# Joined row-tiled runs, one run per kind in the second layer, and another ready rule for an engine's own results

## The chip, the cores and the metric

The kernel runs on one core of a Trainium2 chip. The metric is the time of one execution in microseconds on the device, the median of several runs. The clock of TensorE (PE) has two levels, 1.2 and 2.4 GHz; the profile shows what was granted in each stretch.

## The reference

What is computed is an attention through packed queries, followed by two feed-forward layers:

```python
def sm_attn(qq, kk, vv):
    s = scale * np.matmul(qq, kk.transpose(0, 1, 3, 2))
    s = s - np.max(s, axis=-1, keepdims=True)
    a = np.exp(s)
    a = a / (np.sum(a, axis=-1, keepdims=True) + 1e-09)
    return np.matmul(a, vv)
p_packed = sm_attn(p, k, v)              # q, k, v: (8, 8, 576, 64); p: (8, 8, 32, 64)
out = sm_attn(q, p_packed, p_packed)
x = out.transpose(0, 2, 1, 3).reshape(4608, 512)
h = x @ moe_w_in;  g = h * np.tanh(np.log1p(np.exp(h)));  x = g @ moe_w_out     # 512 -> 2048 -> 512
h = x @ moe2_w_in; g = h - np.tanh(h);                    y = g @ moe2_w_out    # 512 -> 2048 -> 512
```

## The kernel before

The weights come as 64-bit words; ScalarE (ACT) and VectorE (DVE) decode them (`dec_unit`, `dec_split`, `dec_pair`) into float32 and split each into a high and a low part, so that a product of float32 precision is three matmuls (`PASSES`). The first layer's weights are decoded at the start, the second layer's (32 steps, `w2_step` apart) beside the first layer, and parked in DRAM (`w2i_d`, `w2o_d`).

**Attention** (`attention`, per batch b of 8): first scores (`scores`, L484, two calls j), transposes (L511, L513), the packed values (L532, L540), then second scores for each half hf of the 576 tokens (`second_scores`, L558), whose soft-max (L563 to L585, on DVE and ACT) leaves the tile `a2[b, hf]`. `mix(b, g)` (L614, g from 0 to 3) multiplies the packed values into a quarter of the first weights; ACT (L620) and DVE (L622) copy the result from PSUM into the tile `m`. The matmuls of L484, L558 and L614 use 64 rows and 32 columns of the array each, four column tiles beside each other: they are called row-tiled here. Everything after is on the full 128 by 128 array.

**First layer** (`layer1`, 128 steps n): two products of six matmuls of 288 columns (L648, from `m` and `a2`), mish on ACT (L652), the split (L654 on ACT, L655 on DVE into `g`), and 24 matmuls of 288 columns into four accumulators (L666).

**Second layer** (`pair2` and `second`, 72 pairs n in 9 blocks of 512 tokens): seven products of six matmuls of 256 columns (L784), from combinations of blocks of weights (`wm`, two tiles of pool `m` per pair, of 4 and 3 products) and of activations (`yq`), in three PSUM banks `ba`, `bb`, `bc`. Copies (L795 on ACT) and adds (L798 on DVE) make the two hidden tiles `hb`; the last part of the second comes by ACT (L815). `second` takes each through a chain on ACT and DVE (L824 to L840) into `g` and 12 matmuls of 512 columns into the accumulators (L850), evicted by L856 after the sixteenth.

**What sets the order.** `Plan` collects all operations with a key, a duration and their buffers, and `emit` walks through modelled time: each engine takes the ready operation with the lowest key whose buffers are free. The program's order on each engine is what comes out; on the chip each engine follows it, waiting where it must. The ready time of an operation is the end of what it waits for plus `LAT` (0.14 us in the model). All row-tiled and product banks come from one pool `bk` of four PSUM banks. In `pair2` a slot is a fifteenth of `TP`, and the first hidden tile's accumulation stands two `TP` behind its pair.

Of the kernel before, what the change touches and what calls it, by code (L numbers as in the profile page):

```python
# [70 lines left out]
class Plan:  # L71


    LAT = 0.14
    TABLE = 1.3
    WINDOW = 3.413

# [3 lines left out]
    def op(self, eng, dur, fn, key, deps=(), take=(), give=(), table=None):  # L81
        o = Op()
        o.table = table
        o.eng, o.dur, o.fn, o.key = eng, dur, fn, key
        o.takes, o.gives, o.outs, o.ready, o.end = list(take), list(give), [], 0.0, None
        o.wait = 0
        o.seq = len(self.ops)
        for b in o.gives:
            b.left += 1
        for d in set(x for x in deps if x is not None):  # L90
            d.outs.append(o)
            o.wait += 1
        self.ops.append(o)
        return o

    def emit(self):
# [17 lines left out]
        while left:  # L114
# [7 lines left out]
            while moved:  # L122
                moved = False
                for e in engs:
# [9 lines left out]
                    while avail[e]:  # L134
                        ent = heapq.heappop(avail[e])
                        need, turn = {}, True
                        for b in ent[2].takes:
                            for k in (b.kind, b.cap):
                                if k is not None:
                                    need[k] = need.get(k, 0) + 1  # L140
                                    turn = turn and (k.queue is None or k.queue[0] is b)
                        if turn and all(len(k.free) >= n and k not in held_kinds for k, n in need.items()):
                            pick = ent[2]
                            break
                        held_kinds.update(k for k, n in need.items() if len(k.free) < n)
# [44 lines left out]
                    for d in o.outs:  # L190
                        d.wait -= 1
                        d.ready = max(d.ready, o.end)
                        if d.wait == 0:
# [20 lines left out]
def tile_packed_attention_mish_tanhshrink(  # L214
# [70 lines left out]
    def ka(n):  # L285
        return T0 + n * TA
# [84 lines left out]
    w2_st = {}  # L371
    w2_step = (ka(102.7) - ka(11.22)) / 32

# [56 lines left out]
    for i in range(32):  # L430
        key = ka(11.22) + i * w2_step
        if i < 16:
# [9 lines left out]
    a2, a2_rd = {}, {}  # L442
    pp, pp_rd = {}, {}

    def attention(b):
# [3 lines left out]
        if b:  # L449
            spans = [(ka(8.5), ka(12.5), 26) if b == 1 else (ka(16 * b - 16) + 20.02, ka(16 * b - 8) + 8.64, 26)]  # L450
            spans += [(ka(16 * b + 8 * hf - 8) - 13.96, ka(16 * b + 8 * hf) - 21.81, 14) if b > 1 else
                      (ka(12 + 2 * hf), ka(14.5 + 2.5 * hf), 14) for hf in range(2)]
# [23 lines left out]
        def scores(j):  # L476
# [4 lines left out]
            def f():  # L481
                for hf in range(2):
                    for c in range(4):
# [3 lines left out]
                            kk[c][0].tile[64 * j:64 * j + 64, hf * HALF:(hf + 1) * HALF], start=True, stop=True)  # L487
            s1 = op("PE", 1.19, f, key(2), [pt_ld] + [x[1] for x in kk], sc, [pt] + [x[0] for x in kk])
            for hf in range(2):
# [55 lines left out]
        def second_scores(hf):  # L545
# [14 lines left out]
            mm = op("PE", 1.19, f, key(2), [pp_rd[b]] + [x[1] for x in qq], st + [ex, fx, a], [x[0] for x in qq] + [pb])  # L560
            for j in range(2):
# [34 lines left out]
    def mix(b, g):  # L596
# [14 lines left out]
        def f():  # L611
            for j in range(2):
                for c in range(4):
                    T.matmul(pm[j].tile[32 * c:32 * c + 32, :], pp[b].tile[64 * j:64 * j + 64, 32 * c:32 * c + 32],  # L614
                             ws[c][2]()[64 * j:64 * j + 64, :], start=True, stop=True)
        z = op("PE", 1.94, f, k0, [pp_rd[b]] + [w[1] for w in ws], pm + [m], [w[0] for w in ws] + [pp[b]])
        for j in range(2):
# [145 lines left out]
    def pair2(n, sw):  # L763
# [33 lines left out]
        def add(half, tok, bk, c, slot, deps, take, give):  # L797
# [3 lines left out]

        p1 = product(0, 0, ba, [act2[0]], [ba], True)
        s1 = copy(c1, ba, 1, [p1])
        p2 = product(1, 1, bb, [], [bb], True)
        c11 = add(0, 0, bb, c1, 2, [p2, s1], [hb[0]], [bb, c1])
        p5 = product(2, 2, bc, [], [bc], True)
        s5 = copy(c5, bc, 3, [p5])
        p6 = product(3, 5, ba, [p1, s1], [], False)
        sy = copy(cy, ba, 6, [p6])
        p3 = product(4, 6, bc, [p5, s5], [], False)  # L810
        c12 = add(0, 1, bc, cy, 7, [p3, sy, c11], [], [bc, cy])
        p7 = product(5, 9, ba, [p6, sy], [], False)
        c22 = add(1, 1, ba, c5, 10, [p7, s5], [hb[1]], [c5])
# [120 lines left out]
```

## Time and profile before

| | us |
|---|---|
| median of 3 runs | 1515.66 |
| the runs | 1515.66, 1519.52, 1515.3 |
| the profiled execution | 1519.44 |
| its span, first to last instruction | 1517.6 |
| PE busy (matmuls) / weight loads | 1485.4 / 1340.3 |
| DVE busy | 1044.0 |
| ACT busy | 1003.6 |

Matmuls are pipelined, so that a busy PE is not a PE at its peak: how fast it goes is read from the distance between the starts of its groups in the timeline. The idle time of an engine stands in brackets with what ended it. In the table of stages the columns are the stretch, its length, and the busy time with the number of instructions for PE, weight loads (PEld), DVE, ACT and POOL, then the granted share of PE's full clock, the share of the DMA engines and GB/s.

### The profile page before, as it was taken

To read this page: it belongs to the slowest core of one execution; us is meant where nothing else is said; L and a number is where in the kernel's file an instruction comes from. 1 tells how busy PE (TensorE), PEld (TensorE's weight loads), DVE (VectorE), ACT (ScalarE), POOL (GpSimd) and SP (SyncE) were. 2 spreads that over 40 slices of the span, in tenths; PEclk is the share of its full clock that TensorE was granted. 3 is DMA by queue.
4 is the path that set the end of the run, shared out by engine and by line. 5 is a ranking of instruction groups with operands and counts; after the bars stand their busy time and mean duration, and the time that the engine had idled before them with its cause. 6 is when DMAs were issued, how large, how long until landed. Compare 5 with 4: busy or idle time off the path is not lost.

```text
span 1517.6 us, 28157 instructions
## 1 busy us (share of the span) xinstructions
PE 1485.4 (98%) x11112; PEld 1340.3 (88%) x11112; DVE 1044.0 (69%) x1916; ACT 1003.6 (66%) x1992; POOL 0.2 (0%) x4
## 2 busy tenths in 40 slices
PE   4999999999999999999999999999999999999999
PEld 1888899898989989899998898989898898989987
DVE  6978472745646433331488889797988888797876
ACT  5896665666566645543576767676777777676765
POOL 0000000000000000000000000000000000000000
PEclk9899999999999999999999999999999999999999
DMA  8788492655757242312965656565556657575551
GB/s 285 248 301 294 151 300 88 227 189 181 245 167 250 100 148 64 94 62 72 349 213 198 199 174 225 180 224 184 201 195 209 198 181 232 167 231 172 192 194 52
DMA packets 100084, 289.73 MB, mean 191 GB/s; under 512 B 10224, under 2 KB 27760, under 8 KB 90736
## 3 DMA queue, kind: packets, MB, share of 16 engines
q1 hardware_dynamic: 99952, 287.94, 56.4%
q8 instruction: 87, 1.43, 0.4%
q14 instruction: 45, 0.37, 0.1%
HBM read 241.76 MB, written 46.14 MB: 190 GB/s over the span
## 4 chain that ended last, share of the span: by engine, by line
PE 94%; DMA 3%; ACT 2%; DVE 1%; issue 0%; SPq 0%; ACTq 0%
PE acc L850 26%; PE acc L666 26%; PE bk L784 24%; PE bk L648 14%; PE bk L614 2%; PE bk L484 1%; DMA st<-in_w1i 1%; PE bk L532 1%; DMA st<-in_w1o 1%; PE bk L558 1%; DMA x<-in_v 1%; DMA m<-w2i_d 1%; PE bk L511 0%; DMA xw<-w1i_d 0%; ACT st L312 0%
## 5 line engine op out<-in xcount | busy, mean ns | idle before, releaser
L850 PE MATMUL acc<-g,wo 128*128 128x512 f32 x1728 | 444.4, 393 | 0.0
L666 PE MATMUL acc<-g,wo 128*128 128x288 f32 x3072 | 436.6, 296 | 0.4 <-DVE g L655 0.4
L666 PEld LDWEIGHTS acc<-g,wo 128*128 128x128 f32 x3072 | 414.3, 188 | 16.1 <-issue 14.6
L850 PEld LDWEIGHTS acc<-g,wo 128*128 128x128 f32 x1728 | 306.6, 189 | 50.1
L784 PEld LDWEIGHTS bk<-yh,m 128*128 128x128 f32 x2160 | 292.3, 191 | 20.6 <-DVE x L798 2.5
L784 PE MATMUL bk<-yh,m 128*128 128x256 f32 x2160 | 306.7, 284 | 0.1
L648 PEld LDWEIGHTS bk<-a,m 128*128 128x128 f32 x1536 | 212.4, 190 | 35.7 <-ACT a L584 9.4
L648 PE MATMUL bk<-a,m 128*128 128x288 f32 x1536 | 231.2, 300 | 10.5 <-ACT a L584 8.5
L655 DVE TENSOR_TENSOR g<-e,g 128x576 fp32r<-128x576 f32 x128 | 96.6, 755 | 202.7 <-ACT g L654 196.4
L652 ACT ACTIVATE e<-bk 128x288 f32<-128x288 f32 x256 | 103.4, 411 | 140.6 <-PE bk L648 139.9
L835 DVE TENSOR_TENSOR tt<-x,tt 128x512 f32<-128x512 f32 x144 | 99.3, 690 | 68.3 <-ACT tt L828 68.2
L824 ACT ACTIVATE e<-x 128x512 f32<-128x512 f32 x144 | 90.8, 630 | 67.7 <-DVE x L798 66.3
L795 ACT ACTIVATE pc<-bk 128x256 f32<-128x256 f32 x216 | 75.5, 374 | 71.8 <-PE bk L784 70.6
L784 PEld LDWEIGHTS bk<-a,m 128*128 128x128 f32 x864 | 113.3, 191 | 8.7 <-DMA m<-w2i_d 2.9
L784 PE MATMUL bk<-a,m 128*128 128x256 f32 x864 | 115.6, 283 | 2.7 <-DMA m<-w2i_d 2.7
L829 DVE SCALAR_TENSOR_TENSOR xw<-xw,xw 128x512 f32<-128x512 f32 x144 | 99.4, 690 | 25.6 <-ACT xw L827 23.9
L837 DVE COPY_PREDICATED xw<-e,tt 128x512 f32<-128x512 uint32 x144 | 109.3, 759 | 1.6
L798 DVE TENSOR_TENSOR x<-bk,pc 128x256 f32<-128x256 f32 x216 | 90.0, 418 | 24.0 <-PE bk L784 23.6
L839 ACT ACTIVATE g<-xw 128x512 fp32r<-128x512 f32 x144 | 89.4, 621 | 23.9 <-DVE xw L837 23.5
L840 DVE TENSOR_TENSOR g<-xw,g 128x512 fp32r<-128x512 f32 x144 | 98.8, 686 | 7.6 <-ACT g L839 7.6
L825 ACT ACTIVATE xw<-e,c_qb 128x512 f32<-128x512 f32 x144 | 102.3, 711 | 0.0
L833 DVE SCALAR_TENSOR_TENSOR xw<-xw,x 128x512 f32<-128x512 f32 x144 | 98.6, 685 | 0.0
(105 smaller groups left out, 1254.7 us busy)
## 6 DMA issues: line engine op xcount, KB each, us to landing
m<-w2i_d SPq DMA_DIRECT2D x72, 1024.0 KB, 5.1
m<-w2i_d SPq DMA_DIRECT2D x72, 768.0 KB, 4.4
xw<-w1i_d SPq DMA_DIRECT2D x112, 256.0 KB, 4.5
w2i_d<-x SPq DMA_DIRECT2D x56, 256.0 KB, 3.9
x<-in_k SPq DMA_DIRECT2D x32, 288.0 KB, 5.5
x<-in_q SPq DMA_DIRECT2D x64, 144.0 KB, 4.0
y_d<-yv SPq DMA_DIRECT2D x16, 576.0 KB, 4.1
out_t<-x SPq DMA_DIRECT2D x36, 256.0 KB, 5.3
```

What stands on the lines that cost most here:

```text
L648: T.matmul(h.tile[:, :HALF], r(m.tile[:, fc % 4, kc, wl, :]), r(x.tile[:, kc, al, :]), start=(i == 0), stop=(i == 5))
L652: fr.append(op("ACT", a_cost(HALF, True), lambda c=c, h=h: A.activation(e.tile[:, c, :], h.tile[:, :HALF], AF.Mish), kf + 1, [g1] + fr, [e ...
L655: lo = op("DVE", v_cost(576), lambda: V.tensor_tensor(out=r(gt.tile[:, 1]), in0=e.tile, in1=gt.tile[:, 0], op=ALU.subtract), kf + 1.2, [hi ...
L666: T.matmul(ac.tile[:, :HALF], r(wo[fc].tile[:, wl, oc * 128:(oc + 1) * 128]), r(gt.tile[:, gl, c, :]), start=(fc == first and i == 0), sto ...
L784: T.matmul(bk.tile[:, :HB], r(wv[:, kc, wl, :]), r(yq[blk, j].tile[:, kc, yl, :]), start=(first and i == 0), stop=(i == 5), skip_group_che ...
L825: p1 = op("ACT", a_cost(TB, False, True), lambda: A.activation(s1.tile, zz.tile, AF.Sigmoid, bias=c_qb, scale=Q_L), k0 + 0.1, [sq], [s1])
L829: q = op("DVE", v_cost(TB), lambda: V.scalar_tensor_tensor(out=s1.tile, in0=s1.tile, scalar=Q_E, in1=s2.tile, op0=ALU.add, op1=ALU.mult), ...
L833: q = op("DVE", v_cost(TB), lambda: V.scalar_tensor_tensor(out=s1.tile, in0=s1.tile, scalar=Q_A, in1=h.tile, op0=ALU.mult, op1=ALU.mult), ...
L835: d = op("DVE", v_cost(TB), lambda: V.tensor_tensor(out=tt.tile, in0=h.tile, in1=tt.tile, op=ALU.subtract), k0 + 1.3, [th], give=[h])
L837: q = op("DVE", v_cost(TB), lambda: V.copy_predicated(s1.tile, zz.tile.bitcast(U32), tt.tile), k0 + 1.4, [q, d, k], give=[zz, tt])
L840: lo = op("DVE", v_cost(TB), lambda: V.tensor_tensor(out=r(gt.tile[:, 1, :]), in0=s1.tile, in1=gt.tile[:, 0, :], op=ALU.subtract), k0 + 2. ...
L850: T.matmul(ac.tile, r(w2c[fc].tile[:, wl, oc * 128:(oc + 1) * 128]), r(gt.tile[:, gl, :]), start=(fc == 0 and i == 0), stop=(fc == NFC - 1 ...
```

## The change

Five things. `Plan.join` glues one operation to another: a `mix` is run by PE directly ahead of a scores operation (`mate`), as one operation that takes the buffers of both. 24 of the 32 mixes get such a mate: from batch 2 on those with g under 2 the second scores of their own batch, and from batch 1 on those with g of 2 and 3 the first scores of the next batch. The attention's keys move to fit (`spans`). In `pair2` the slots are spread so that seven products of three pairs stand in a row and then 24 matmuls of L850. In `emit` a result counts as ready for its own engine when the engine is free, without `LAT`; and ACT holds back an operation that needs another function table while one of the present table is ready or due within `SOON`. The second weights' decoding starts at step 17 of the first layer instead of 11.22.

```diff
+    def join(self, o, dur, fn, key, deps=(), take=(), give=()):
+        back = o.fn
+        def both():
+            fn()
+            back()
+        o.fn, o.key, o.dur = both, key, o.dur + dur
...
+                        if e == "ACT" and ent[2].table not in (None, table) and any(
+                                x[2].table == table and x[0] < t + self.SOON for x in pend[e]):
+                            turn = False
...
-                        d.ready = max(d.ready, o.end)
+                        d.ready = max(d.ready, free[e] if d.eng == e else o.end)
...
-    w2_step = (ka(102.7) - ka(11.22)) / 32
+    w2_step = (ka(102.7) - ka(17)) / 32
...
-            spans = [(ka(8.5), ka(12.5), 26) if b == 1 else (ka(16 * b - 16) + 20.02, ka(16 * b - 8) + 8.64, 26)]
-            spans += [(ka(16 * b + 8 * hf - 8) - 13.96, ka(16 * b + 8 * hf) - 21.81, 14) if b > 1 else
+            spans = [(ka(8.5), ka(12.5), 26) if b == 1 else
+                     (ka(16 * b - 18) - 2.4, ka(16 * b - 18) + 28.7, 26)]
+            spans += [(ka(16 * b - 6 + 2 * hf) - 3.0, ka(16 * b - 6 + 2 * hf) + 18.0, 14) if b > 1 else
...
-        z = op("PE", 1.94, f, k0, [pp_rd[b]] + [w[1] for w in ws], pm + [m], [w[0] for w in ws] + [pp[b]])
+        args = (f, k0, [pp_rd[b]] + [w[1] for w in ws], pm + [m], [w[0] for w in ws] + [pp[b]])
+        mate = None if b == 0 or b == 1 and g < 2 else mm2[b, g] if g < 2 else mm1.get((b + 1, g - 2))
+        z = op("PE", 1.94, *args) if mate is None else plan.join(mate, 1.5, *args)
...
-                             k0 - 26 + 6 * i, [w2_st[p, j] for j in range(j0, j1)] + [sw], [wm[i]]))
+                             k0 - 26 + 11 * i, [w2_st[p, j] for j in range(j0, j1)] + [sw], [wm[i]]))
...
-        p1 = product(0, 0, ba, [act2[0]], [ba], True)
+        p1 = product(0, 2, ba, [act2[0]], [ba], True)
...
-        p4 = product(6, 12, ba, [p7, c22], [], False)
+        p4 = product(6, 30, ba, [p7, c22], [], False)
...
-        second(blk, p, hb[0], [c11, c12], ks(8), k0 + 2 * TP, (3, 4, 7, 8))
-        second(blk, p + 8, hb[1], [c21, c22], ks(14), k0 + 2 * TP, (10, 11, 13, 14))
+        second(blk, p, hb[0], [c11, c12], ks(20), k0, (41, 42, 43, 44))
+        second(blk, p + 8, hb[1], [c21, c22], ks(32), k0, (52, 53, 54, 55))
```

The lines move by up to 30: L484 becomes L510, L558 L584, L614 L640, L648 L677, L666 L695, L784 L813, L850 L880, L563 L589, L585 L611, L622 L651, L798 L827.

PE in the middle of the second layer, before (L784 are products, L850 accumulations):

```order
L784 MATMUL bk_17290<-yh_16778,m_17114 128x256 x6
L784 MATMUL bk_17311<-yh_16723,m_17168 128x256 x6
L850 MATMUL acc_0_17117<-g_17189,wo_8791 128x512 x3
L850 MATMUL acc_0_17122<-g_17189,wo_8791 128x512 x3
L784 MATMUL bk_17290<-yh_16787,m_17168 128x256 x6
L850 MATMUL acc_0_17079<-g_17253,wo_8815 128x512 x3
L850 MATMUL acc_0_17087<-g_17253,wo_8815 128x512 x3
L850 MATMUL acc_0_17117<-g_17253,wo_8815 128x512 x3
L784 MATMUL bk_17290<-yh_16797,m_17168 128x256 x6
L850 MATMUL acc_0_17122<-g_17253,wo_8815 128x512 x3
```

and after (L813 and L880):

```order
L813 MATMUL bk_17104<-yh_16779,m_17111 128x256 x6
L813 MATMUL bk_17221<-yh_16736,m_17100 128x256 x6
L813 MATMUL bk_17338<-a_2_15855,m_17217 128x256 x6
L813 MATMUL bk_17265<-yh_16685,m_17228 128x256 x6
L813 MATMUL bk_17359<-a_0_16668,m_17217 128x256 x6
L813 MATMUL bk_17221<-yh_16757,m_17228 128x256 x6
L813 MATMUL bk_17382<-yh_15954,m_17217 128x256 x6
L880 MATMUL acc_0_17059<-g_17290,wo_8816 128x512 x3
L880 MATMUL acc_0_17069<-g_17290,wo_8816 128x512 x3
L880 MATMUL acc_0_17075<-g_17290,wo_8816 128x512 x3
L880 MATMUL acc_0_17080<-g_17290,wo_8816 128x512 x3
```

Products and accumulations, which took turns after one to three groups, now stand as seven products and eight accumulation groups; the number of runs of L784 falls from 281 to 73, and of L850 alike.

PE in the first layer, a mix of batch 3 before (L614), between an accumulation and the next step's products:

```order
L666 MATMUL acc_0_3527<-g_3734,wo_1022 128x288 x3
L614 MATMUL bk_3932<-xw_3678,ppb_3359 32x512
L614 MATMUL bk_3932<-xw_3711,ppb_3359 32x512
L614 MATMUL bk_3932<-xw_3789,ppb_3359 32x512
L614 MATMUL bk_3932<-xw_3800,ppb_3359 32x512
L614 MATMUL bk_3933<-xw_3678,ppb_3359 32x512
L614 MATMUL bk_3933<-xw_3711,ppb_3359 32x512
L614 MATMUL bk_3933<-xw_3789,ppb_3359 32x512
L614 MATMUL bk_3933<-xw_3800,ppb_3359 32x512
L648 MATMUL bk_3957<-a_0_3439,m_3464 128x288 x6
```

and the end of one after (L640), with the second scores (L584) that follow it:

```order
L640 MATMUL bk_3474<-xw_2673,ppb_3013 32x512
L640 MATMUL bk_3474<-xw_2685,ppb_3013 32x512
L640 MATMUL bk_3474<-xw_2801,ppb_3013 32x512
L640 MATMUL bk_3474<-xw_2808,ppb_3013 32x512
L584 MATMUL bk_3468<-x_3149,ppb_3013 32x288
L584 MATMUL bk_3468<-x_3155,ppb_3013 32x288
L584 MATMUL bk_3468<-x_3164,ppb_3013 32x288
L584 MATMUL bk_3468<-x_3176,ppb_3013 32x288
L584 MATMUL bk_3469<-x_3149,ppb_3013 32x288
L584 MATMUL bk_3469<-x_3155,ppb_3013 32x288
L584 MATMUL bk_3469<-x_3164,ppb_3013 32x288
L584 MATMUL bk_3469<-x_3176,ppb_3013 32x288
```

The two row-tiled pieces stand without a full-array matmul between them. Over the program PE goes from a scores or mix run back to the full array 58 times before and 35 times after.

DVE at the start, from the sums of the first soft-max to its result `a` (before; L319, L321 and L334 are decoding, L622 the copy of a mix):

```order
L576 TENSOR_REDUCE s_0_336<-ex_271 128x18
L622 TENSOR_TENSOR m_295<-bk_293,m_295 128x4x128
L578 TENSOR_SCALAR s_0_336<-s_0_336 128x18
L622 TENSOR_TENSOR m_295<-bk_294,m_295 128x4x128
L580 RECIPROCAL s_0_336<-s_0_336 128x18
L334 TENSOR_TENSOR wo_338<-rr_305,wo_338 128x512
L581 TENSOR_TENSOR ex_271<-ex_271,s_0_336 128x576
L321 SCALAR_TENSOR_TENSOR so_316<-st_282,so_316 128x512
L583 STREAM_TRANSPOSE fx_272<-ex_271 128x576
L622 TENSOR_TENSOR m_322<-bk_320,m_322 128x4x128
L334 TENSOR_TENSOR wo_358<-so_316,wo_358 128x512
L585 TENSOR_TENSOR a_0_273<-fx_272,a_0_273 128x2x288
```

and after:

```order
L602 TENSOR_REDUCE s_0_308<-ex_267 128x18
L604 TENSOR_SCALAR s_0_308<-s_0_308 128x18
L606 RECIPROCAL s_0_308<-s_0_308 128x18
L607 TENSOR_TENSOR ex_267<-ex_267,s_0_308 128x576
L609 STREAM_TRANSPOSE fx_268<-ex_267 128x576
L651 TENSOR_TENSOR m_286<-bk_285,m_286 128x4x128
L345 SCALAR_TENSOR_TENSOR wo_280<-st_188,wo_280 128x512
L611 TENSOR_TENSOR a_0_269<-fx_268,a_0_269 128x2x288
```

Operations of the soft-max follow each other directly; four others between these went behind it (ten others stood between L563 and L585 before, four stand between L589 and L611 after).

## Rows read from the trace of the kernel before

**Rows 1.** Table of stages: stretch, length, busy time of each engine, PE clock, DMA.

```profile
39.36:100.00 60.64, 58.67 (x448) 52.46 (x449) 52.67 (x91) 53.82 (x105) 0.00 (x0) 0.95 0.74 259
140.00:747.73 607.73, 607.73 (x5342) 562.43 (x5341) 294.42 (x548) 353.65 (x687) 0.00 (x0) 1.00 0.50 168
747.73:764.18 16.45, 13.74 (x100) 13.33 (x98) 9.26 (x19) 11.57 (x24) 0.00 (x0) 0.90 0.93 339
764.18:1502.24 738.06, 738.06 (x4608) 663.73 (x4607) 626.79 (x1142) 526.71 (x1069) 0.00 (x0) 1.00 0.58 193
```

**Rows 2.** Timeline of PE, first layer: start, length, engine, line, matmuls.

```profile
300.17 3.35 PE L666 MATMUL acc<-g,wo 128*128 128x288 f32 x24
303.36 1.77 PE L648 MATMUL bk<-a,m 128*128 128x288 f32 x12
305.05 0.72 PE L558 MATMUL bk<-x,ppb 64*32 64x288 f32 x16
305.70 3.44 PE L666 MATMUL acc<-g,wo 128*128 128x288 f32 x24
309.07 1.09 PE L614 MATMUL bk<-xw,ppb 64*32 64x512 f32 x16
310.09 1.88 PE L648 MATMUL bk<-a,m 128*128 128x288 f32 x12
```

**Rows 3.** Timeline of PE, where a mix and scores already follow each other.

```profile
131.25 1.09 PE L614 MATMUL bk<-xw,ppb 64*32 64x512 f32 x16
132.14 0.69 PE L558 MATMUL bk<-x,ppb 64*32 64x288 f32 x16
132.76 1.46 PE L666 MATMUL acc<-g,wo 128*128 128x288 f32 x9
```

**Rows 4.** Timeline of PE, second layer, around the change of a block.

```profile
1008.00 1.55 PE L850 MATMUL acc<-g,wo 128*128 128x512 f32 x6
1009.38 1.59 PE L784 MATMUL bk<-yh,m 128*128 128x256 f32 x12
1010.82 1.55 PE L850 MATMUL acc<-g,wo 128*128 128x512 f32 x6
...
1012.92 1.55 PE L850 MATMUL acc<-g,wo 128*128 128x512 f32 x6
1014.40 0.98 PE L784 MATMUL bk<-yh,m 128*128 128x256 f32 x6
1015.22 1.55 PE L850 MATMUL acc<-g,wo 128*128 128x512 f32 x6
```

**Rows 5.** Timeline at the end: the last accumulations and the last chain's end.

```profile
1502.24 11.75 PE L850 MATMUL acc<-g,wo 128*128 128x512 f32 x51
...
1508.86 0.69 DVE L840 TENSOR_TENSOR g<-xw,g 128x512 fp32r<-128x512 f32 x1 [0.76 <-ACT g L839]
```

**Rows 6.** Timeline of PE and of DVE at the start.

```profile
17.98 2.83 PE L532 MATMUL bk<-x,a1T 128*32 128x64 f32 x80
...
22.43 0.43 DVE L317 TENSOR_SCALAR wo<-st 128x512 uint32<-128x512 uint32 x1 [1.26 <-DMA st<-in_w1i]
...
23.75 0.28 DVE L537 TENSOR_TENSOR ppn<-bk,sm 128x128 f32<-128x128 f32 x1
...
28.29 0.84 DVE L563 STREAM_TRANSPOSE ex<-bk 128x288 f32<-128x288 f32 x2
29.05 0.65 DVE L321 SCALAR_TENSOR_TENSOR wo<-st,wo 128x512 uint32<-128x512 uint32 x1
29.63 0.74 DVE L571 TENSOR_REDUCE m<-ex 128x18 f32<-128x576 f32 x1
...
39.36 0.61 PE L648 MATMUL bk<-a,m 128*128 128x288 f32 x1 [8.53 <-ACT a L584]
```

**Rows 7.** Timeline of PE, its wait at the second layer's start.

```profile
758.99 1.40 PE L784 MATMUL bk<-a,m 128*128 128x256 f32 x6 [2.65 <-DMA m<-w2i_d]
```

**Rows 8.** Page, groups of instructions: busy, mean ns of one, idle before.

```profile
L798 DVE TENSOR_TENSOR x<-bk,pc 128x256 f32<-128x256 f32 x216 | 90.0, 418 | 24.0 <-PE bk L784 23.6
```

More of the change, by code (lines that the diff above doesn't have):

```diff
@@ L75 @@
     TABLE = 1.3
+    SOON = 1.0
     WINDOW = 3.413
@@ L93, in op @@
         self.ops.append(o)
+        return o
+    def join(self, o, dur, fn, key, deps=(), take=(), give=()):
[4 more added lines that the diff above has]
+        o.fn, o.key, o.dur = both, key, o.dur + dur
+        for b in give:
+            b.left += 1
+        o.takes += take
+        o.gives += give
+        new = set(x for x in deps if x is not None) - set(d for d in self.ops if o in d.outs)
+        for d in new:
+            d.outs.append(o)
+            o.wait += 1
         return o
@@ L430, in tile_packed_attention_mish_tanhshrink @@
     for i in range(32):
-        key = ka(11.22) + i * w2_step
+        key = ka(17) + i * w2_step
         if i < 16:
@@ L443, in tile_packed_attention_mish_tanhshrink @@
     pp, pp_rd = {}, {}
+    mm1, mm2 = {}, {}
     def attention(b):
@@ L487, in f @@
                             kk[c][0].tile[64 * j:64 * j + 64, hf * HALF:(hf + 1) * HALF], start=True, stop=True)
-            s1 = op("PE", 1.19, f, key(2), [pt_ld] + [x[1] for x in kk], sc, [pt] + [x[0] for x in kk])
+            s1 = mm1[b, j] = op("PE", 1.19, f, key(2), [pt_ld] + [x[1] for x in kk], sc, [pt] + [x[0] for x in kk])
             for hf in range(2):
@@ L559, in f @@
                                  qq[c][0].tile[64 * j:64 * j + 64, :HALF], start=True, stop=True)
-            mm = op("PE", 1.19, f, key(2), [pp_rd[b]] + [x[1] for x in qq], st + [ex, fx, a], [x[0] for x in qq] + [pb])
+            mm = mm2[b, hf] = op("PE", 1.19, f, key(2), [pp_rd[b]] + [x[1] for x in qq], st + [ex, fx, a], [x[0] for x in qq] + [pb])
             for j in range(2):
@@ L800, in add @@
                 ks(slot), deps, take, give)
-        p1 = product(0, 0, ba, [act2[0]], [ba], True)
[L803 to L813, printed above, removed]
-        p4 = product(6, 12, ba, [p7, c22], [], False)
+        p1 = product(0, 2, ba, [act2[0]], [ba], True)
+        s1 = copy(c1, ba, 3, [p1])
+        p2 = product(1, 4, bb, [], [bb], True)
+        c11 = add(0, 0, bb, c1, 5, [p2, s1], [hb[0]], [bb, c1])
+        p5 = product(2, 6, bc, [], [bc], True)
+        s5 = copy(c5, bc, 7, [p5])
+        p6 = product(3, 16, ba, [p1, s1], [], False)
+        sy = copy(cy, ba, 17, [p6])
+        p3 = product(4, 18, bc, [p5, s5], [], False)
+        c12 = add(0, 1, bc, cy, 19, [p3, sy, c11], [], [bc, cy])
+        p7 = product(5, 20, ba, [p6, sy], [], False)
+        c22 = add(1, 1, ba, c5, 21, [p7, s5], [hb[1]], [c5])
+        p4 = product(6, 30, ba, [p7, c22], [], False)
         c21 = op("ACT", a_cost(HB, True), lambda: A.activation(hb[1].tile[:, :HB], ba.tile[:, :HB], AF.Copy),
-                 ks(13), [p4, c22], give=[ba])
-        second(blk, p, hb[0], [c11, c12], ks(8), k0 + 2 * TP, (3, 4, 7, 8))
-        second(blk, p + 8, hb[1], [c21, c22], ks(14), k0 + 2 * TP, (10, 11, 13, 14))
+                 ks(31), [p4, c22], give=[ba])
+        second(blk, p, hb[0], [c11, c12], ks(20), k0, (41, 42, 43, 44))
+        second(blk, p + 8, hb[1], [c21, c22], ks(32), k0, (52, 53, 54, 55))
     def second(blk, fc, h, rd, k0, k1, slots):
```

## The prediction

> **What bounds the kernel now.** I read the table of stages first. From 140.00 to 747.73 us PE has no idle time, and none from 764.18 to 1502.24; DVE and ACT have room in both stages [rows 1]. So what the change does to DVE and ACT there is worth nothing by itself, and what counts is how densely PE's matmuls follow each other. That is read from the starts in PE's timeline, not from busy time. Three stretches are different: the start, where PE waits 8.53 us for the first soft-max result and takes up the first layer at 39.36 [rows 6]; the stretch to 100.00, where PE is busy 58.67 of 60.64 us while DVE is busy for 87% and ACT for 89% [rows 1]; and the start of the second layer, with a wait of 2.65 us for weights [rows 7].
>
> Durations come from the profiled execution, 1519.44 us, which is 3.8 above the median of 1515.66. I work out differences and take them from the median.
>
> **Part 1, joined runs.** What does a row-tiled run cost beside its own time? 24 matmuls of L666 take 3.19 us where nothing row-tiled stands next to them (300.17 to 303.36). Between L558 and L614, the 24 take 3.37 (305.70 to 309.07) [rows 2]. So one way out of a row-tiled run and one way in cost 0.18 us together. The runs themselves last 0.65 (305.05 to 305.70) and 1.02 (309.07 to 310.09); two apart so cost 0.65 + 1.02 + 2 x 0.18 = 2.03. Where they already follow each other, both take 1.51, from 131.25 to 132.76 [rows 3]; with one way in and out that is 1.69. A join saves 0.34 us, and the order shows 23 returns to the full array fewer: 23 x 0.34 = **7.8 us**, on PE's path. Twelve of the joins are with first scores (L484), a pair that no row shows. If these save only the way in and out, 0.18, the sum is 11 x 0.34 + 12 x 0.18 = 5.9; that is the lower bound; the upper is 23 x 0.36 = 8.3, since the rows round to 0.01.
>
> Against it stands a new wait: a joined run takes all four banks of `bk`, and the next L648 needs one back. The order puts 6 to 24 matmuls of L666 between, so at least 6 x 0.133 = 0.8 us. Two transposes, which free two banks, take 0.84 [rows 6], and a first bank is back after half of that if DVE is free; it is busy for half of this stage [rows 1], so some will be late. I take 0.5 us in all. The bounds are 0, and 24 x 0.25 = 6 us, if each join meets a late operation.
>
> **Part 2, one run per kind.** Is a change of kind dear? Six of L850 take 1.38 us (1008.00 to 1009.38), and twelve of L784 1.44, 0.120 each [rows 4]. In the run of 51 at the end one L850 takes 0.227: 11.75 less the 0.40 of a single one, over 50 [rows 5]; the 0.40 is the 1.55 of the six less five steps of 0.23 [rows 4]. Six at that pace are 1.363. A run of L850 costs 0.017 more than its matmuls in a long run, and 208 runs go away: 208 x 0.017 = **3.5 us**. The rows round to 0.01, so that 1.5 and 5.5 are the bounds.
>
> Could a long run go faster still? The paces of 256 and of 512 columns differ by 0.107, so that 0.013 of each matmul are beside its columns [rows 4, 5]. If long runs lost that, 4752 matmuls would give 62 us. The run of 51 still has it, and so it is only a rival, below. The page *TensorE: Matmul & The Clock Gate* of the Trainium skill (section Back-to-back issue gap) speaks for that rival: an isolated matmul, it says, follows the last after N/2.4 + 2.5 ns, which makes 109 and 216 here; an estimate by that page takes 52 us off instead of the 3.5, but the 0.227 in the run of 51 disagrees with it, and the measurement decides.
>
> Each period now needs its banks in one row of products. The tightest is the seventh product: its bank comes back by the add after the fourth, two products (1.43 us) earlier. The add takes 0.418 [rows 8], DVE is busy 85% of the stage [rows 1]; 1.0 us of slack remains, more than one DVE operation of those shown. I take nothing. The chain from hidden tile to `g` had 25 slots of cover and has 20 or 21, about 14 us; at the end of the program it takes 7.3 from the last product to L840's end (1502.24 to 1509.55) [rows 5], so it fits. Nothing gained or lost there, nor at the block changes, where two steps are 0.10 longer each [rows 4].
>
> **Part 3, the end.** Behind the last product PE had 51 matmuls, 11.6 us, which hid the chain of 7.3. Now 24 stand there, 5.5 us ahead of those that need the last chain: 12 of the 36 left. PE waits 7.3 - 5.5 = 1.8, and about 0.2 to take up again: **+2.0 us**. Bounds 1.5, and 4 if the chain before it delays the last.
>
> **Part 4, the start.** Between L563 and L585 stood ten operations of decoding and mixes and now four; six go behind, at 0.6 each (29.05 to 29.63): 3.6 us. Ahead of L563, the values of L532 were there at 20.81, but L537 came at 23.75, behind decoding that had waited for its weights until 22.43, and L563 at 28.29 [rows 6]. Now L537 stands ahead of that weight, and L563 behind three decoding operations less; some 3.6 us more. PE can start 7.2 us earlier. But nothing is removed: from that result to the last copy of the fourth mix DVE has 84 operations after and 74 before, and it is nearly full there. Ten at 0.6 give back 6 of the 7.2, where PE had been waiting for these copies in this stretch. The gain lies between 1.2 and 7.2. Second weights decoded later take work off DVE late in this stretch, and part of PE's 1.97 us without work [rows 1] may go. I take **3.5 us**, with 0 and 8 as bounds. Fewer function tables are loaded, ten by the order; ACT is off the path past 100 us, so I count nothing for them, and nothing for the new ready rule except the order.
>
> **Part 5, the second layer's start.** The wait of 2.65 us is for the third pair's weights, in the buffer of the first pair's four products [rows 7]. Now that buffer takes a piece of three quarters of the size, needed one product (0.72) later. About 1.2 us would be left. The granted clock of this stage is 0.90, part of it at the lower of the two levels [rows 1], which is 1.6 us of 16.45; a shorter wait may save that. Together up to 3.0; new waits may come from the spread start of pairs. I take **2.0**, bounds 0 and 4.
>
> **Sum.** -7.8 + 0.5 - 3.5 + 2.0 - 3.5 - 2.0 = -14.3 us: 1505.1 for the profiled execution, and 1515.66 - 14.3 = **1501.4** against the median.
>
> **Rivals.** First, the start keeps its whole lead (7.2 instead of 3.5) and the second layer starts without a wait (3.0 instead of 2.0): 1496.7, and 1493 with the other gains at their best. For it speaks that PE's waits up to 100 us are short, against it that DVE is nearly full there. Second, the joins' banks come late and give back 6 instead of 0.5, with the start at 1.2: 1509. That DVE is half idle in the first layer speaks against it [rows 1]. Third, slower: the row of seven products waits for its banks. Each wait costs like the two longer steps at a block, 0.2 us [rows 4]. One a period is 72 x 0.2 = 14.4 us, 1515.8, no change; two a period are 28.8, **1530**. It decides from one wait a period on, and from 1.3 on the kernel would be measurably slower. DVE's 85% speaks for it, the slack above against it. Fourth, long runs lose what a matmul has beside its columns: 62 us instead of 3.5, 1443; the run of 51 speaks against it. By the gap in the page of the Trainium skill it would be 1453. Fifth, the joins save nothing, since row-tiled runs wait for each other anyway: 1509; the 1.51 us for both speak against it [rows 3].
>
> **How the numbers follow.** Forecast 0.61 (1496 to 1506), the first rival 0.12, the second and fifth 0.13 together, one wait a period 0.06, two a period 0.06, the long-run gap 0.02. A measurement can tell about 0.3% from no change, 4.5 us, so faster means under 1511.1: 0.61 + 0.12 + 0.11 + 0.02 = 0.86. Same: 0.08, slower 0.06. The range for 8 in 10 leaves out the third and fourth rival and the far end of the others: 1493 to 1510.
>
> **What would show it.** The second layer's middle should have runs of 42 and 24 matmuls and a period of 42 x 0.120 + 24 x 0.227 + 0.02 = 10.51 us, against 10.56 with four changes, and no waits on L827. A joined run with second scores should last 1.5 us, with 0.18 around it. PE should take up L677 at about 32 us, and at the end wait some 2 us for L870. If the period is longer than before, the third rival holds; if PE idles behind joined runs, the second; if the idle time before 100 us grows by as much as the start came earlier, part 4 was too high.

## The result and the profile after

| | before | after |
|---|---|---|
| median, beside each other (us) | 1517.04 | 1527.12 |
| the profiled execution | 1519.44 | 1524.89 |
| its span | 1517.6 | 1523.1 |

The ratio is 1.0064, 95% interval [1.0051, 1.0076]: the changed kernel is slower by 0.64%, some 10 us, where 14 us less were forecast. The two profiled executions lie closer together than the medians, 5.5 us in span, so the stages below account for 5.5.

The page's line on the chain that ended last, before:

```profile
PE 94%; DMA 3%; ACT 2%; DVE 1%; issue 0%; SPq 0%; ACTq 0%
```

and after:

```profile
PE 71%; DVE 13%; ACT 9%; DMA 4%; issue 2%; SPq 0%; DVEq 0%; ACTq 0%
```

Before, the end hung on PE nearly all the way. After, 22% of it hangs on DVE and ACT. Where that is, the table of stages of after shows (stretch, length, busy time of PE, PEld, DVE, ACT, POOL, granted clock, DMA), to be held against [rows 1]:

```profile
31.07:100.00 68.93, 63.39 (x480) 55.97 (x481) 61.38 (x103) 59.33 (x113) 0.00 (x0) 0.98 0.80 271
140.00:746.53 606.53, 598.74 (x5328) 560.42 (x5327) 303.68 (x557) 342.35 (x680) 0.00 (x0) 1.00 0.51 170
746.53:760.01 13.48, 12.06 (x99) 11.69 (x97) 6.56 (x14) 11.12 (x23) 0.00 (x0) 1.00 0.86 321
760.01:1509.24 749.23, 741.51 (x4621) 668.60 (x4620) 628.05 (x1148) 530.50 (x1070) 0.00 (x0) 1.00 0.53 191
```

PE takes up the first layer at 31.07 instead of 39.36: the lead of 8.3 us came, a little more than the 7.2 of part 4. But length less PE's busy time is 5.5 us up to 100 (2.0 before), 7.8 to the end of the first layer and 7.7 in the second; in the last two PE had no idle time at all in [rows 1]. What PE waited for, after (engine, line and what it waited for: us in total, times, longest), first from 140 to 735, then from 735 on; left out are waits of 0.5 us in all in the first stretch and of 1.2 at the program's end:

```profile
PE bk L677 <- DVE m L651: 3.7, 5, 0.8
PE bk L677 <- DVE ex L589: 3.4, 3, 1.8
...
PE bk L813 <- DVE x L827: 4.7, 7, 0.7
PE acc L880 <- ACT x L886: 3.0, 8, 0.6
PE bk L813 <- ACT xw L857: 1.4, 1, 1.4
```

A wait costs more than its idle time. At 1002.62 below, the idle time is 0.66, the product starts 0.82 late, and its six matmuls then take 0.82 instead of 0.72.

**At the start.** The lead is gone by step 8 of the first layer (a step has twelve matmuls of L677): it begins at 76.35 us, and at 76.50 before. PE takes up the products early, but then waits for the next soft-max result, which held nothing up before. Timeline of PE, after:

```profile
52.96 0.40 PE L677 MATMUL bk<-a,m 128*128 128x288 f32 x1 [1.20 <-ACT a L610]
54.62 1.81 PE L677 MATMUL bk<-a,m 128*128 128x288 f32 x6 [1.26 <-DVE a L611]
```

And 171 matmuls stand ahead of the first product before, 155 after: the 16 of a mix have moved behind it.

**Behind a joined run.** Timeline of after, PE and DVE:

```profile
463.66 1.09 PE L640 MATMUL bk<-xw,ppb 64*32 64x512 f32 x16
464.55 0.69 PE L584 MATMUL bk<-x,ppb 64*32 64x288 f32 x16
465.17 1.45 PE L695 MATMUL acc<-g,wo 128*128 128x288 f32 x9
466.12 0.43 DVE L341 TENSOR_SCALAR so<-st 128x512 uint32<-128x512 uint32 x1 [3.17 <-DMA w2o_d<-so]
...
467.31 0.69 DVE L345 SCALAR_TENSOR_TENSOR so<-st,so 128x512 uint32<-128x512 uint32 x1
467.93 0.48 DVE L589 STREAM_TRANSPOSE ex<-bk 128x288 f32<-128x288 f32 x1
468.46 1.06 PE L677 MATMUL bk<-a,m 128*128 128x288 f32 x6 [1.84 <-DVE ex L589]
```

The joined run lasts 1.51 us (463.66 to 465.17), as part 1 had it. It holds all four banks. The transposes that free two of them (L589) could begin at 465.2, but on DVE they stand behind a decoding step of the second weights (L341 to L345) which itself waited 3.17 us for its scratch tile to be written out. PE has nine matmuls, 1.2 us, and then waits. The three waits for L589 (3.4 us) are of this kind; at one of them, before 187.81, the decoding ahead had not itself waited.

The five waits for L651, the copy of a mix (3.7 us), are not. They stand behind joined runs with first scores, and decoding has no part in them: on DVE the chain of a soft-max (L604 to L609) and the reductions of the scores (L516, L519) stand ahead of the copies, and in four of the five the first copy also waits 0.28 us for ACT's (L649). Timeline of after, DVE and PE:

```profile
299.11 0.79 DVE L516 TENSOR_REDUCE mx<-bk 128x1 f32<-128x288 f32 x2
...
300.43 1.29 DVE L651 TENSOR_TENSOR m<-bk,m 128x512 fp32r<-128x512 f32 x2 [0.28 <-ACT m L649]
...
301.26 0.90 PE L677 MATMUL bk<-a,m 128*128 128x288 f32 x5 [0.84 <-DVE m L651]
```

**In the second layer.** Timeline of after at the beginning of a block, PE and then DVE:

```profile
1001.08 0.88 PE L813 MATMUL bk<-yh,m 128*128 128x256 f32 x6
1002.62 0.98 PE L813 MATMUL bk<-yh,m 128*128 128x256 f32 x6 [0.66 <-DVE x L827]
1003.44 5.63 PE L880 MATMUL acc<-g,wo 128*128 128x512 f32 x24
...
1000.34 0.69 DVE L766 TENSOR_TENSOR yv<-yv 128x512 f32<-128x512 f32 x1
1000.95 0.69 DVE L870 TENSOR_TENSOR g<-xw,g 128x512 fp32r<-128x512 f32 x1
1001.55 0.69 DVE L766 TENSOR_TENSOR yv<-yh,yv 128x512 f32<-128x512 f32 x1
1002.15 0.42 DVE L827 TENSOR_TENSOR x<-bk,pc 128x256 f32<-128x256 f32 x1
...
1003.42 0.69 DVE L863 SCALAR_TENSOR_TENSOR xw<-xw,x 128x512 f32<-128x512 f32 x1
1004.02 0.68 DVE L865 TENSOR_TENSOR tt<-x,tt 128x512 f32<-128x512 f32 x1
1004.74 0.78 DVE L867 COPY_PREDICATED xw<-e,tt 128x512 f32<-128x512 uint32 x1
```

The seventh product waits for the add L827, the wait that part 2 took as not there. It comes at most once in a block (seven times in nine blocks), where DVE also prepares the next block's activations (L766): when the fourth product ended, at about 1000.4, three operations of 0.60 us stood ahead of the add. A second wait comes at each change of block, for the eviction of an accumulator (L886). From the first product of one block to that of the next it is 85.6 us, against 84.6 before; forecast was 84.2.

The last three rows show what turned out to matter. L865 starts 0.60 us after L863, whose result it doesn't take. L867 takes L865's result and starts 0.72 after it. In all 144 such pairs of after, which follow each other directly, the distance is 0.71 to 0.74. In the kernel before, such pairs mostly have another operation between them; in the kernels with the new slots and the old ready rule (experiments 2 and 10) 48 follow each other directly.

### The profile page after: what moved, and what is told of

The parts are those of the page before. It is cut to its first block, busy times and chain, and to the rows that moved or that the text cites. A ratio compares the mean times of both kernels' runs of the same rounds, so it can differ in the third digit from the quotient of the medians.

```text
span 1523.1 us, 28030 instructions
## 1 busy us (share of the span) xinstructions
PE 1478.4 (97%) x11112; PEld 1343.6 (88%) x11112; DVE 1049.5 (69%) x1916; ACT 996.2 (65%) x1982; POOL 0.2 (0%) x4
## 4 chain that ended last, share of the span: by engine, by line
PE 71%; DVE 13%; ACT 9%; DMA 4%; issue 2%; SPq 0%; DVEq 0%; ACTq 0%
PE acc L695 21%; PE acc L880 19%; PE bk L813 16%; PE bk L677 11%; PE bk L640 1%; DVE tt L865 1%; DVE xw L859 1%; DVE xw L863 1%; DMA w2o_d<-so 1%; ACT g L869 1%; ACT xw L855 1%; DVE xw L867 1%; DVE x L827 1%; DMA st<-in_w1o 1%; ACT e L854 1%
## 5 line engine op out<-in xcount | busy, mean ns | idle before, releaser
L695 PE MATMUL acc<-g,wo 128*128 128x288 f32 x3072 | 440.3, 296 | 0.4 <-DVE g L684 0.3
L695 PEld LDWEIGHTS acc<-g,wo 128*128 128x128 f32 x3072 | 415.7, 188 | 16.2 <-issue 14.1
L880 PE MATMUL acc<-g,wo 128*128 128x512 f32 x1728 | 408.6, 391 | 4.2 <-ACT x L886 3.0
L880 PEld LDWEIGHTS acc<-g,wo 128*128 128x128 f32 x1728 | 319.0, 188 | 71.4 <-ACT x L886 6.4
L813 PE MATMUL bk<-yh,m 128*128 128x256 f32 x2160 | 296.8, 284 | 6.1 <-DVE x L827 4.7
L813 PEld LDWEIGHTS bk<-yh,m 128*128 128x128 f32 x2160 | 279.7, 191 | 14.3 <-DVE x L827 6.8
L677 PE MATMUL bk<-a,m 128*128 128x288 f32 x1536 | 233.0, 299 | 18.6 <-ACT a L610 6.8
L677 PEld LDWEIGHTS bk<-a,m 128*128 128x128 f32 x1536 | 213.3, 190 | 28.4 <-ACT a L610 8.8
L869 ACT ACTIVATE g<-xw 128x512 fp32r<-128x512 f32 x144 | 90.3, 627 | 197.7 <-DVE xw L867 162.7
L827 DVE TENSOR_TENSOR x<-bk,pc 128x256 f32<-128x256 f32 x216 | 84.0, 417 | 88.6 <-PE bk L813 88.6
L813 PE MATMUL bk<-a,m 128*128 128x256 f32 x864 | 127.0, 283 | 0.0
L870 DVE TENSOR_TENSOR g<-xw,g 128x512 fp32r<-128x512 f32 x144 | 99.2, 689 | 37.4 <-ACT g L869 37.4
L813 PEld LDWEIGHTS bk<-a,m 128*128 128x128 f32 x864 | 114.0, 192 | 0.0
L867 DVE COPY_PREDICATED xw<-e,tt 128x512 f32<-128x512 uint32 x144 | 110.0, 764 | 5.0
L863 DVE SCALAR_TENSOR_TENSOR xw<-xw,x 128x512 f32<-128x512 f32 x144 | 98.7, 685 | 0.0
L865 DVE TENSOR_TENSOR tt<-x,tt 128x512 f32<-128x512 f32 x144 | 98.6, 685 | 0.0
L683 ACT ACTIVATE g<-e 128x576 fp32r<-128x576 f32 x128 | 87.9, 687 | 4.0
```

The costliest lines, as they stand in the source:

```text
L677: T.matmul(h.tile[:, :HALF], r(m.tile[:, fc % 4, kc, wl, :]), r(x.tile[:, kc, al, :]), start=(i == 0), stop=(i == 5))
L695: T.matmul(ac.tile[:, :HALF], r(wo[fc].tile[:, wl, oc * 128:(oc + 1) * 128]), r(gt.tile[:, gl, c, :]), start=(fc == first and i == 0), sto ...
L813: T.matmul(bk.tile[:, :HB], r(wv[:, kc, wl, :]), r(yq[blk, j].tile[:, kc, yl, :]), start=(first and i == 0), stop=(i == 5), skip_group_che ...
L863: q = op("DVE", v_cost(TB), lambda: V.scalar_tensor_tensor(out=s1.tile, in0=s1.tile, scalar=Q_A, in1=h.tile, op0=ALU.mult, op1=ALU.mult), ...
L865: d = op("DVE", v_cost(TB), lambda: V.tensor_tensor(out=tt.tile, in0=h.tile, in1=tt.tile, op=ALU.subtract), k0 + 1.3, [th], give=[h])
L867: q = op("DVE", v_cost(TB), lambda: V.copy_predicated(s1.tile, zz.tile.bitcast(U32), tt.tile), k0 + 1.4, [q, d, k], give=[zz, tt])
```

## The experiments

Each is one edit against the kernel after, or against the one before where its text says so. Ratios are to the kernel before on the same chip.

**1. The old slots.**

```diff
-        p1 = product(0, 2, ba, [act2[0]], [ba], True)
+        p1 = product(0, 0, ba, [act2[0]], [ba], True)
...
-                             k0 - 26 + 11 * i,
+                             k0 - 26 + 6 * i,
```

> The kernel after, with the second layer's slots and the key of the weights' second tile as they were before; all else as after. Theory S (the slots): the 6.9 us that the second layer lost (766.1 to 773.0 from its first product to the end of its last accumulation) come from the row of seven products on four banks and from the block change behind a run of 24 accumulations. Then this stretch is back at 766 and the time is 1527.1 - 6.9 = 1520. Theory R (the ready rule): ACT and DVE are planned closer than they run, whatever the slots, so that the stretch stays at 770 to 773 and the time is 1524 to 1527.

1530.37 us, ratio 1.0089 [1.0071, 1.0107]: against theory S, and 3 us above what theory R gave. A block takes 85.5 us with the old slots too, and the stretch of 773.0 us takes 777.3. The slots are not the cause; they make the kernel faster.

**2. The old ready rule.**

```diff
-                        d.ready = max(d.ready, free[e] if d.eng == e else o.end)
+                        d.ready = max(d.ready, o.end)
```

> The kernel after, with the ready rule of before (a result is ready for its own engine 0.14 us after its end, in the plan); all else as after. Both theories: the first product of the first layer stands behind as many operations of DVE as before, so it starts at 39 us instead of 31, of which some 3.5 us come back as shorter waits up to 120 us: +5. Theory S: the second layer stays at 772 to 773 us and the waits behind the joined runs (9.8 us between 120 and 746) stay, so the time is 1527 + 5 = 1532. Theory R: both go, the second layer takes 763 to 766 and the first has no waits, 1527 + 5 - 8 - 10 = 1514.

1506.5 us, ratio 0.9935 [0.992, 0.9949]: theory R, and 7 us better than it gave. (The 9.8 us of waits in the expectation are 7.6 in the list above.) One line turns 0.64% slower into 0.65% faster; this version beats both kernels. A block takes 84.2 us, the page's chain hangs on PE for 90%, and all that PE waits for from 140 us on is 2.4 us to 735 and, at the very end, 1.2 us for the last chain (L868, L869).

Timeline of DVE in this kernel, the same chain (L862, L864 and L866 are L863, L865 and L867 of after):

```profile
987.12 0.68 DVE L862 SCALAR_TENSOR_TENSOR xw<-xw,x 128x512 f32<-128x512 f32 x1
987.73 0.68 DVE L864 TENSOR_TENSOR tt<-x,tt 128x512 f32<-128x512 f32 x1
988.33 0.68 DVE L771 TENSOR_TENSOR a<-yv,a 128x512 fp32r<-128x512 f32 x1
988.93 0.76 DVE L866 COPY_PREDICATED xw<-e,tt 128x512 f32<-128x512 uint32 x1
```

An activation split stands in the gap, all four start 0.60 or 0.61 apart, and the pair costs nothing extra.

**3. No joins**, and the old `spans`.

```diff
-        z = op("PE", 1.94, *args) if mate is None else plan.join(mate, 1.5, *args)
+        z = op("PE", 1.94, *args)
```

> The kernel after without joins and with the attention's keys of before; all else as after. Theory J (the joined run takes all four banks, and what frees them stands on DVE behind the second weights' decoding): the waits of 9.8 us between 120 and 746 us go, the 23 joins cost 7.5 us back, so the first layer's stretch gets 2 us shorter and the time is 1525. Theory D (the waits come from the later decoding or the ready rule and not from the joins): the waits stay, and the time is 1527 + 7.5 = 1534.5.

1524.41 us, ratio 1.0055 [1.004, 1.007]: theory J, in its time and its waits. Its reason, the decoding ahead on DVE, holds for the transposes' 3.4 us of the 7.6 and not for the copies' 3.7. From 140 to 735 the trace shows no wait of PE at all, and with the waits the joins' gain is gone. The second layer waits as in after (4.7 us for the add, 2.9 for the eviction).

**4. The ready rule alone**, on the kernel before.

> The kernel before with the new ready rule alone. Theory S: the rule brings the start forward by 8 us, of which some 3.5 are given back up to 120 us, and costs nothing elsewhere: second layer 766 us, no waits from 140 to 746, time 1517 - 5 = 1512. Theory R: the start comes forward in the same way, but the second layer loses 4 to 7 us and waits show in the first layer, so that the time is 1517 to 1522.

1530.83 us, ratio 1.0098 [1.0081, 1.0115]: slower than either theory gave, and theory R's place: the second layer's blocks take 85.6. The lead came (PE takes up the first layer at 31.97) and was gone by 140 us, in eight kinds of waits; from there to 735 PE doesn't wait, so that theory R was wrong on the first layer: there the rule costs where a joined run meets it. ACT in this kernel shows the same spacing as DVE:

```profile
1006.97 0.62 ACT L825 ACTIVATE e<-x 128x512 f32<-128x512 f32 x1
1007.62 0.72 ACT L826 ACTIVATE xw<-e,c_qb 128x512 f32<-128x512 f32 x1
1008.25 0.61 ACT L828 ACTIVATE xw<-e 128x512 f32<-128x512 f32 x1
1008.77 0.61 ACT L829 ACTIVATE tt<-x 128x512 f32<-128x512 f32 x1
```

L826 takes L825's result and starts 0.65 after it; L829 doesn't take L828's and starts 0.52 after.

**5. The rule with its price.** Is it the 0.12 us themselves, or that the plan doesn't know of them?

```diff
+                        if e in ("ACT", "DVE"):
+                            if last.get(e) is not None and o in last[e].outs and t <= last[e].end:
+                                dur += self.LAT
+                            last[e] = o
```

> The kernel after, ready rule and all, but the plan charges 0.14 us more for an operation of DVE or ACT that takes the result of the one directly ahead of it on its engine. In the trace of after such a pair starts 0.72 us apart on DVE (L865 at 1004.02, L867 at 1004.74) where others of its kind start 0.60 apart. In the order 133 of the 144 pairs L865 to L867 still stand directly behind each other (48 with the old rule). Theory T (time: the harm is that the plan takes DVE and ACT to be earlier than they are, so that PE is sent to a bank that is not free): PE finds no waits in the second layer, a block of eight pairs takes 84.2 to 84.6 us, the start stays at 31 to 32, and the time is 1506.5 - 1.4 = 1505, the 1.4 being the lead over the kernel with the old rule at step 16 (127.99 against 129.43). Theory O (order: the pairs themselves make DVE and ACT too slow): a block stays at 85.3 us or more and the time at 1520 or more.

1507.85 us, ratio 0.9942 [0.9925, 0.9959]: theory T, 3 us above its 1505. One of its conditions failed: PE takes up the first layer at 34.22 us, not at 31 to 32. A block takes 84.2 us. The pairs are still there, and in the whole second layer PE waits for the add (L832 here) once:

```profile
PE bk L818 <- DVE x L832: 0.2, 1, 0.2
```

Timeline of PE and DVE at the beginning of a block (L818, L885, L870 and L872 are L813, L880, L865 and L867 of after):

```profile
991.85 0.88 PE L818 MATMUL bk<-yh,m 128*128 128x256 f32 x6
992.57 2.91 PE L885 MATMUL acc<-g,wo 128*128 128x512 f32 x12
995.32 0.88 PE L818 MATMUL bk<-yh,m 128*128 128x256 f32 x6
...
989.03 0.68 DVE L870 TENSOR_TENSOR tt<-x,tt 128x512 f32<-128x512 f32 x1
989.74 0.76 DVE L872 COPY_PREDICATED xw<-e,tt 128x512 f32<-128x512 uint32 x1
```

DVE's pair is 0.71 apart as in after, but the plan now counts that time, and lets twelve accumulations go ahead of the seventh product. PE follows a written order: where the plan is wrong, it stands.

**6 and 7. The rule for one engine**, DVE and then ACT.

```diff
-                        d.ready = max(d.ready, free[e] if d.eng == e else o.end)
+                        d.ready = max(d.ready, free[e] if d.eng == e == "DVE" else o.end)
```

> The kernel after with the new ready rule for DVE alone (ACT and PE by the old one). Theory V: DVE's pairs carry the harm, since the waits in both layers name DVE (L827, L589, L651): time 1524 to 1527, a block 85.3 to 85.6 us, PE takes up the first layer at 31 to 32 us. Theory A: ACT's pairs (125 from L681 to L683, 72 from L854 to L855) carry it, since the chain to L869 is what comes late: a block 84.2, time 1505.

1520.44 us, ratio 1.0027 [1.0016, 1.0038]; a block 85.5.

> The kernel after with the new ready rule for ACT alone. In both theories PE takes up the first layer at 38.7 us as with the old rule, as DVE's order there is that of the old rule. Theory V: a block of 84.2 us, time 1506 to 1508. Theory A: a block of 85.3 to 85.6, time 1518 to 1527.

1510.21 us, ratio 0.9954 [0.9939, 0.9969]; a block 84.6. Against 1506.5 without the rule, DVE's part is 14 us and ACT's 4, together 18 of the 20 between this and the kernel after. Theory V held for the most part: DVE's part is by far the larger, but the first kernel is 4 us below its range and the second 2 above. Its reason, the waits that name DVE, doesn't hold in the second layer: with the rule on DVE alone PE doesn't wait for the add there, but 6.0 us for ACT's eviction at the block change.

**8. The rule for the start alone.**

```diff
-                        d.ready = max(d.ready, free[e] if d.eng == e else o.end)
+                        d.ready = max(d.ready, free[e] if d.eng == e and t < 50 else o.end)
```

> The kernel after with the new ready rule for the first 50 us of the plan alone, the old rule behind. PE takes up the first layer at 31 to 32 us, and a block of the second layer takes 84.2. If the lead at the start is given back as in the kernel after (1.4 us of 7.6 left at step 16) the time is 1505; if it stays, 1499; in either case both kernels are beaten.

1510.36 us, ratio 0.9959 [0.9945, 0.9974]: faster than both kernels but slower than experiment 2; I had expected 1505 or less. The table of stages from the first matmul of the first layer to its step 16, here and then in experiment 2:

```profile
31.30:131.12 99.82, 94.43 (x791) 82.23 (x791) 79.83 (x138) 81.39 (x154) 0.00 (x0) 0.95 0.81 277
```

```profile
38.66:129.43 90.77, 89.43 (x772) 80.50 (x773) 75.11 (x130) 76.60 (x146) 0.00 (x0) 0.96 0.83 281
```

PE starts 7.4 us earlier and is at step 16 1.7 us later, with 5.4 us idle instead of 1.3. The start's lead is worth nothing: by step 8 it is gone (76.16 against 75.86). In all fourteen kernels of this document step 8 begins between 73.9 and 76.9 us, whether PE takes up the first layer at 31 or at 39. Why the lead is worth less than nothing stays open.

**9 to 11. Single parts on the kernel before.** The joins with their keys; the slots with the weights' key; the later decoding.

> The kernel before with the joins and the attention's new keys alone. By part 1 of the prediction -7.8 + 0.5 = -7.3: 1508.4 of 1515.7. If the joined runs find their banks late even with the old ready rule (second rival of the prediction), -7.8 + 6: 1514. In the kernel with all parts but the rule, PE waits 2.4 us between 120 and 735, so that I expect some 2 us given back: 1510.

1519.72 us, ratio 1.002 [1.0011, 1.003], slower where 1510 was expected. PE waits 6.2 us from 140 to 735, in ten waits; 2.5 of it are for the banks that DVE gives back (1.6 for transposes, 0.9 for a mix's copy), the rest for other results of ACT and DVE. If each wait costs 0.26 beside its idle time, as the one at 1002.62 in after did (0.92 for 0.66), the ten come to 8.8 us, more than the 7.8 of the joins; that is an estimate. The longest wait for a transpose has the cause seen in after; timeline of PE and DVE:

```profile
384.11 1.06 PE L689 MATMUL acc<-g,wo 128*128 128x288 f32 x6
384.47 0.43 DVE L335 TENSOR_SCALAR so<-st 128x512 uint32<-128x512 uint32 x1 [1.14 <-DMA w2o_d<-so]
...
385.54 0.84 DVE L583 STREAM_TRANSPOSE ex<-bk 128x288 f32<-128x288 f32 x2
386.07 1.19 PE L671 MATMUL bk<-a,m 128*128 128x288 f32 x7 [0.89 <-DVE ex L583]
```

> The kernel before with the second layer's new slots and the weights' new key alone. By parts 2, 3 and 5 of the prediction -3.5 + 2.0 - 2.0 = -3.5: 1512.2, with no PE waits between 800 and 1480. If the seven products in a row need what the new rule or the table hold gives, waits on L798 show and it is 1515 or slower. The kernel with all parts but the rule took 5.3 us less than before from the first product to the last accumulation's end: 1510.4.

1512.22 us, ratio 0.997 [0.9959, 0.9982], in line with parts 2, 3 and 5. That the time is met so closely is luck: the kernel before took 1516.86 beside it instead of 1515.7, so that the gain is 4.6 us and not 3.5, and the interval, 2.7 to 6.2, holds both. A block takes 84.2, and the two waits left of the second layer are its start and its end:

```profile
757.48 2.41 PE L784 MATMUL bk<-yh,m 128*128 128x256 f32 x18 [0.88 <-DMA m<-w2i_d]
...
1504.30 0.50 PE L851 MATMUL acc<-g,wo 128*128 128x512 f32 x1 [1.02 <-ACT g L840]
1505.02 2.80 PE L851 MATMUL acc<-g,wo 128*128 128x512 f32 x11 [0.23 <-DVE g L841]
```

> The kernel before with the second weights decoded from step 17 alone. The kernel with all parts but the rule reaches step 16 of the first layer 5.3 us earlier than before though it starts at the same time. If that is DVE's and ACT's work taken out of the stretch to 100 us, this kernel does the same and takes 1510 to 1512. If it is only attention moved behind step 16, it is 1515.7, no change (the prediction counted no separate term for it).

1518.4 us, ratio 1.0011 [1.0001, 1.002]: no change that counts. Step 16 comes at 129.89 instead of 134.69 and the lead is gone by the layer's end (the second begins at 749.21 instead of 747.86).

**12. The old rule without the table hold.**

> The kernel after with the old ready rule and without the hold for function tables (61 loads of tables in the order instead of 51). The prediction counts nothing for tables: 1506.5 as with the hold. If ACT's ten loads of 1.3 us are in the way of the joined runs or of the start, 1508 to 1515.

1507.78 us, ratio 0.9936 [0.9921, 0.9951]: the hold is worth nothing that can be told. This kernel is joins, slots and decoding on the kernel before. Its first layer, from its first matmul to the second layer's first product, takes 703.5 us; with the joins but the early decoding (experiment 9) it takes 710.3, with the later decoding but no joins (11) 711.0, and before 708.5. Neither pays alone; together they take 5.0 off. Part of the 5.0 may be chance: the profiled execution of before is 2.6 us longer than its median beside these runs. What the later decoding spares the joins was not looked at further than the wait shown in experiment 9, and stays open.

## Why the prediction was wrong

**The step that failed** is half a sentence at the end of part 4: "nothing for the new ready rule except the order". I had read the rule as a choice among orders. It is a statement about time: that an engine can begin an operation when the one that makes its input ends. The trace of before could have contradicted it, had I compared starts: independent operations of DVE start 0.60 apart though each is recorded as lasting 0.68 or 0.69, dependent ones 0.72. Timeline of DVE, before: L837 takes L833's result, but not that of L743.

```profile
1491.36 0.69 DVE L833 SCALAR_TENSOR_TENSOR xw<-xw,x 128x512 f32<-128x512 f32 x1
1492.08 0.76 DVE L837 COPY_PREDICATED xw<-e,tt 128x512 f32<-128x512 uint32 x1
...
1006.70 0.68 DVE L743 TENSOR_TENSOR a<-yv,a 128x512 fp32r<-128x512 f32 x1
1007.31 0.77 DVE L837 COPY_PREDICATED xw<-e,tt 128x512 f32<-128x512 uint32 x1
```

The page *Perfetto Trace Analysis* of the Trainium skill (section DVE / Act Engine Instruction (TENSOR_ADD, Activation, etc)) describes what the starts show: the next instruction may begin its reads when the last has finished executing, ahead of the acknowledged write that ends its record, while a semaphore update goes out only with that acknowledgement and has still to be propagated. The trace agrees: in after L865 starts 0.09 before the recorded end of L863, L867 0.04 behind that of L865. In experiments 2 and 5 the old latency, or a price for the pair, gives 21 and 19 us back; alone on the kernel before, the rule costs 15 (experiment 4).

The rest of the sum, held against kernels without the rule where there is one:

- **Part 1, joins, 7.8 and 0.5 back.** The size of a join was right: 1.51 us for both pieces, 23 returns fewer. The pair with first scores, which no row showed, takes 1.99 in after where its pieces take 1.02 and 1.10 apart in before; with the 0.18 that is 0.31 a join, and 7.5 in all. The wait was wrong, even without the rule: 2.4 us in experiment 2, 6.2 with the joins alone, 7.6 in after. I had asked whether DVE is busy half the time; what counts is what stands on DVE ahead of the transposes and copies that free the banks, and whether that itself waits. The second rival named this wait; its price (6) fits after and the joins alone in size, in the latter partly by luck, since only 2.5 of the 6.2 are for these banks.
- **Part 2, runs, 3.5.** Right: 0.40 us a block by experiment 10, 3.6 in nine blocks. The step "I take nothing" for the seventh product's bank holds in experiments 2 and 10 and fails with the rule. The third rival had the mechanism, but neither the rate nor the price: one wait in a block, not in a period, and 0.9 us instead of 0.2, with some 0.5 more at the block change. A block takes 85.6 instead of the 84.2 of experiment 10, and the second layer 773.0 instead of 761.1: 12 us. A mean load of 85% had hidden the one place in a block where DVE has the next block's activations in hand as well.
- **Part 3, the end, 2.0.** Right within 0.3: in experiment 10 PE takes up the last twelve matmuls 1.2 us late, and the first of them, with a second wait of 0.23, takes 0.72 to the next instead of 0.23: 1.7 in all.
- **Part 4, the start, 3.5.** The lead was right (8.3 in after, 7.4 in experiment 8), its worth was not: 0, the lower bound, or less. All of it is given back, where I had taken 3.5 of 7.2 as left.
- **Part 5, 2.0.** The mechanism was right and the size too small: the stretch's wait falls from 2.65 [rows 7] to 1.4 in after (there for ACT) and 0.88 in experiment 10, and the granted clock is 1.00 in after, where it was 0.90. From the first product to the first accumulation, 96 matmuls, it is 16.3 us before, 13.5 in after and 13.0 in experiment 10: 2.8 and 3.3, the "up to 3.0" of the prediction.

So the sum without part 4 and with 2.4 for the joins' waits is -8.9. Experiment 2 has 1506.5 against 1515.92 beside it: -9.4. That these meet doesn't show that each part earned its share. Alone on the kernel before, the joins cost 2.9 us, the slots gain 4.6 and the later decoding costs 1.5, together a gain of 0.2; experiment 12 has all three and gains 9.1. Some 9 us come only where they stand together, for which the prediction has no term; the cause is open.

In after itself, against before: 8.3 us of lead at the start, of which 1.3 are left where the second layer begins, since the joins' gain and more went into waits; and 6.9 lost in the second layer (766.1 to 773.0 from first product to last accumulation), 12 of waits less what the runs and the start gave. That is the 5.5 us of the spans.

## What to carry to other kernels

Where a plan writes the order of engines that don't reorder, a wrong 0.12 us in it is not paid as 0.12 us on an engine with room to spare, but as a wait on the engine that bounds: price a dependent pair on one engine from the starts in the trace before trusting a new rule. A batch of work that takes every buffer of a pool should be judged by what stands ahead of its releasers in their queues, and whether that waits itself, not by how busy their engine is. Read loads where they peak, not as a mean over a stage.

## What was unexpected of the hardware

Two operations of DVE on 512 columns start 0.60 us apart when independent and 0.71 to 0.74 when the second reads the first's result (the 144 pairs of after); on ACT 0.52 to 0.54 and 0.65 to 0.67 (the operations behind L825 and L828 in experiment 4). And PE loses more than the idle time shown at a wait: 0.92 us for 0.66 idle with products of 256 columns.
